# A new order for the 1297 steps of a hand-ordered attention and MLP kernel

## The chip, the cores and the metric

The kernel runs on one core of a Trainium2 chip. Times are device microseconds (us) of one execution. Before the change the median of three runs is 326.21 us (325.22 to 327.37).

## What is computed

Causal attention in a sliding window of 64 positions (8 batches, 8 heads, 576 positions, 64 wide), and behind it an MLP over all 4608 tokens, whose activation is `h - tanh(h)`:

```python
scores = scale * np.matmul(q, k.transpose(0, 1, 3, 2))
rel = pos[:, None] - pos[None, :]
scores = np.where((rel >= 0) & (rel < 64), scores, -1000000000.0)
attn = softmax(scores)
x = (attn @ v).transpose(0, 2, 1, 3).reshape(4608, 512)
h = x @ w_in            # 512 x 2048
out = (h - np.tanh(h)) @ w_out
```

Inputs and output are float32; the kernel multiplies in bfloat16 and adds up in float32.

## The kernel before

The kernel is one string, `PLAN`, of 1297 words. Each word is a step, that is a call of a small function; `play` calls them from left to right, so each engine gets its instructions in the order of the words. A letter behind a step names its engine: `a` ACT (ScalarE), `v` DVE (VectorE), `p` POOL (GpSimd), `s` SP (SyncE, which only issues DMAs). Engines run side by side and wait for each other by semaphores alone; within an engine, and within a queue of DMA issues, a step that waits holds up all behind it.

Heads are worked on in pairs, four to a batch: pair g belongs to batch g // 4. The MLP takes the 4608 tokens in 9 chunks of 512. So attention of later batches lies between the matmuls of the MLP for earlier tokens. The steps:

- Loads. `lk.g`, `lq.g`: K and Q rows of a pair, 144 KB as they arrive (L106); the first two go through SP as float32, the others through GpSimd, which converts on the way. `lv.b.r.h`, `lt.b`: V of one head, 64 KB (L145, L140). `LV.b.i`: V rows of 128 positions, all heads, 128 KB (L158). `LQ.b`: all Q of a batch, 576 KB (L112). `lr.b.i.h`: K rows of 128 positions (L174). `wi.0` to `wi.2`: w_in in parts for the hidden blocks 0 to 3, 4 to 7 and 8 to 15 (512, 512 and 1024 KB, L187). `wo.0` to `wo.3`: w_out, 512 KB each (L195).
- Q and K to channels on partitions. Batches 0 to 2: `ck.g`, `cq.g` reorder or convert the rows, `Fp.g`, `Ep.g` transpose them on PE (six matmuls of 96 columns, L258), `Fc.g` copies K out of PSUM, `Ea.g` and `Eb.g` copy the two heads of Q (L86 on ACT, L88 on DVE). From batch 3 on K is transposed by a DMA that SP issues (`tk.b.i`, L179); from batch 6 on Q too, by way of DRAM: `cz.g` spreads the rows on GpSimd (L126), `bo.g` writes them (L131), `td.g` reads them back transposed (L136). The buffers `qT`, which hold a pair's queries, are two: `td.g` waits for the scores of pair g-2.
- Attention. `Rp.g.n.bank`: three score matmuls of 128 columns into a PSUM bank (L286; the first four pairs add the mask with a product of its own, L275). `Rx`: exp on ACT (L291). `M.g`: the mask by a product on DVE (L295), for later pairs; the mask lies in PSUM bank 6. `za`, `zb`, `Z.b`: copies of V between the halves of the partitions. `P.g`, `D.g`: PV and normalisation of one pair (L307, L347, L349); `PP.g`, `DR`, `DN`: the same for two pairs, in banks 5 to 7 (L320, L328, L340). `Xp`, `Xc`: the result transposed on PE and copied to the chunk (L355), or from batch 3 on by a DMA, `Y.b` (L374).
- MLP. `H`: one hidden block of a chunk, four matmuls (L385), into banks 0 and 1 in turn; `A`: tanh on ACT (L392); `G`: the subtraction on DVE (L398), which frees the bank; `W`: a quarter of a down-projection of 128 tokens, four matmuls (L417); `O`: copy to SBUF and output DMA on SP.
- `U.n`: n matmuls of 512 columns of zeros, which keep PE busy (L222). `i`, `h`, `n`, `N`: identity and masks, on GpSimd first. `u`, `mv`, `mq`, `mt`, `mk`, `z`: cleared buffers.

Of the kernel before, what the change touches and what calls it, by code (L numbers as in the profile page):

```python
# [15 lines left out]
def kernel(  # L16
# [48 lines left out]
    NR, NPT, NROW = 2, 4, 3  # L65
    hidden_by_product = range(4)
# [181 lines left out]
    def tr(g, which, bank):  # L248
        tp = ps[:, bank, :].bitcast(BF16)[:, 0:E * P].rearrange("c (e p) -> c e p", e=E)
        if (g, which) not in rows:  # L250
            src = stage.pop((g, which))
            for h in range(2):
                for e in range(E):
                    nc.tensor.transpose(tp[64 * h:64 * h + 64, e, :], src[:, h, 64 * e:64 * e + 64], ident[:P, :P])
            return
        src = rows.pop((g, which)).rearrange("p e h d -> p e (h d)")
        for e in range(E):
            nc.tensor.transpose(tp[:, e, :], src[:, e, :], ident[:P, :P])  # L258

    def put(g, which, bank, eng):  # L260
        t = ps[:, bank, :].bitcast(BF16)[:, 0:E * P].rearrange("c (e p) -> c p e", e=E)
        if which == "c":
            move(eng, qp[g % NR].rearrange("c (p e) -> c p e", e=E), t)
        elif which == "k":
            move(eng, kT[g % NR][:, 64:].rearrange("c (p e) -> c p e", e=E), t)
        else:
            h = "ab".index(which)
            r = slice(64 * h, 64 * h + 64)
            move(eng, qT[g % NR].rearrange("c h (p e) -> c h p e", e=E)[r, h], t[r])

    def scores(g, grp, bank):
        sp = ps[:, bank, 0:384].rearrange("p (i q) -> p i q", i=3)
        first = g not in hidden_by_product
        if not first:
            nc.tensor.matmul(sp, ident, hide.rearrange("p h t -> p (h t)").unsqueeze(1).to_broadcast([128, 3, 128]),  # L275
                             start=True, stop=False)
        for i in range(3):
            j = 3 * grp + i
            kt = kT[g % NR] if g // NP not in K_BY_DMA else kw[g // NP % 2][:, g % NP]
            if g // NP in BY_HEAD:  # L280
                for h in range(2):
                    r = slice(64 * h, 64 * h + 64)
                    nc.tensor.matmul(sp[:, i, r], kt[r, 64 * j:64 * j + 128], qp[g % NR][r, 64 * j:64 * j + 64],
                                     start=first, stop=first or (i == 2 and h == 1))
                continue
            nc.tensor.matmul(sp[:, i, :], kt[:, 64 * j:64 * j + 128], qT[g % NR][:, :, 64 * j:64 * j + 64],  # L286
                             start=first, stop=first or i == 2)
# [9 lines left out]
    def pv_banks(g):  # L297
        return ps[:, 4:8:3, :] if g < NP and g % 2 else ps[:, 5:7, :]
# [83 lines left out]
    def hp_mm(c, m):  # L382
        hp = ps[:, m % 2 if c > 1 else m % 3, :]
        for ki in range(4):
            nc.tensor.matmul(hp, w_in_tile(ki, m),  # L385
                             chunk_tile(c)[:, :, ki % 2, 64 * (ki // 2):64 * (ki // 2) + 64],
# [53 lines left out]
    def step(what):  # L440
        i = count[what]
        count[what] += 1
        c, m = divmod(i, 4 if what == "O" else M)
        return c, m

    def first_layer():
        c, m = step("H")
        hidden[c, m] = hp_mm(c, m)

    def tanh():  # L450
        k = step("A")
        hidden[k] = squash(hidden[k])

    def subtract():
        c, m = step("G")
        g_sub(c, m, *hidden.pop((c, m)))
# [11 lines left out]
        Fc=lambda g, k, e: put(g, "k", k, e), Ea=lambda g, k, e: put(g, "a", k, e), Ec=lambda g, k, e: put(g, "c", k, e), Eb=lambda g, k, e: put(g, "b", k, e),  # L468
        Rp=scores, Rx=probs, M=masking, za=cross_low, zb=cross_high, Z=cross_rows,
# [3 lines left out]
    def play(script):  # L473
# [5 lines left out]
        lk.0.s lq.0.s i h n u U.6 mq.1 mv.1 mv.0 ck.0.v cq.0.a mq.0 mt.0 Fp.0.2 U.2 Fc.0.2.a Ep.0.3 U.2  # L479
        Eb.0.3.v Ea.0.3.a Rp.0.0.0 lk.2.p lq.2.p lq.1.p lk.3.p cq.2.a Rx.0.0.0 Rp.0.1.1 U.2 Rp.0.2.0  # L480
        lv.0.2.1 lt.0 lv.0.2.0 mt.1 ck.2.v Fp.2.2 Ep.2.3 Fc.2.2.v Eb.2.3.v lk.1.p ck.1.v lk.4.p lv.0.3.0
        lv.0.1.0 lq.3.p lq.5.p lv.0.1.1 lv.0.3.1 lk.5.p Rx.0.2.0 Ea.2.3.a Rx.0.1.1 cq.1.a lv.0.0.1 lv.0.0.0
        lq.4.p lk.6.p wi.0 wi.1 lq.6.p wi.2 lq.7.p lv.1.1.0 lv.1.1.1 lt.1 lv.1.0.0 lv.1.0.1 lk.7.p wo.0 N
        U.5 Rp.2.2.0 Rp.2.1.1 Rx.2.1.1 Rx.2.2.0 Ep.1.3 Eb.1.3.a Fp.1.2 U.1 Rp.2.0.0 U.2 Rx.2.0.0 ck.3.a
        Ea.1.3.v Fc.1.2.v ck.4.v za.0.2.v zb.0.2.v Rp.1.0.1 Rx.1.0.1 Rp.1.1.0 P.2 Rp.1.2.1 cq.3.a Fp.3.2
        Ep.3.3 D.2 Rx.1.2.1 Eb.3.3.a Ea.3.3.a Rx.1.1.0 Fp.4.3 za.0.1.v cq.5.v zb.0.1.v Fc.3.2.v Rp.3.2.1
        Rx.3.2.1 P.1 Rp.3.1.0 ck.5.v zb.0.3.v za.0.3.v zb.0.0.v za.0.0.v Rp.3.0.1 Fc.4.3.a Rx.3.1.0 Rx.3.0.1
        D.1 Ep.5.3 Eb.5.3.a Ea.5.3.a P.0 P.3 D.0 Fp.5.3 Fc.5.3.a Xp.0.0.1.2 Xc.0.0.1.2.a D.3 Xp.0.1.0.3
        Rp.5.2.4 Xp.0.1.1.2 Xc.0.1.0.3.a Rx.5.2.4 Xp.0.0.0.3 Rp.5.1.4 Xc.0.0.0.3.a cq.4.v ck.6.v
        Xc.0.1.1.2.v Ep.4.3 Eb.4.3.a Rx.5.1.4 H H Rp.5.0.4 A Ea.4.3.a Rx.5.0.4 H A G G M.5 Rp.4.0.4 H  # L490
# [89 lines left out]
```

## Time and profile before

| | |
|---|---|
| Median of 3 runs | 326.21 us |
| Profiled execution | 328.84 us |
| its span, first to last instruction | 327.1 us |
| 144 up-projection blocks, L385, PE busy | 142.1 us |
| 35 full down-projections, L417, PE busy | 136.2 us |
| subtraction L398, DVE | 98.4 us in 144 instructions |
| tanh L392, ACT | 85.3 us in 144 |
| exp L291, ACT | 46.1 us in 96 |
| HBM | 36.70 MB read, 11.80 MB written |

"Busy" is the time that at least one instruction of the engine was under way, so a busy PE need not be at its best rate: four matmuls of 512 columns in a row take 0.86 us where nothing holds them up. A DMA's issue takes its queue's engine some time (0.64 to 0.8 us on GpSimd), and it lands later. The chain of waits, the work that ended last, traced back from the end, lies on PE for 71% of the span and on DMA for 14%.

### The profile page before, as it was taken

Reading aid. Unit: us, or ns where it says so; the run is one execution under the profiler, and the core shown is the slowest. Engines: PE = TensorE matmul, PEld = TensorE weight load, DVE = VectorE, ACT = ScalarE, POOL = GpSimd, SP = SyncE. Lnnn points to the kernel's source line nnn. Section 1 sums busy time; section 2 is a strip of 40 time slices with the busy share of each in tenths; the row PEclk is TensorE's granted clock in tenths of the full one; section 3 lists DMA queues with packets and bytes.
Section 4 is the critical chain, followed back from the end, with each engine's and each line's share of the span. In section 5 each row is a group of like instructions: output and inputs, shape, how many; then the busy total and the mean of one; then the engine's idle time right before and its main releaser. Section 6 shows DMA issues by size and latency. Waiting matters only on the chain.

```text
span 327.1 us, 5992 instructions
## 1 busy us (share of the span) xinstructions
PE 307.7 (94%) x2343; PEld 167.8 (51%) x2343; DVE 196.3 (60%) x337; ACT 175.3 (54%) x326; POOL 112.2 (34%) x166
## 2 busy tenths in 40 slices
PE   7858999999899999999999995999999999999995
PEld 2546555556555545555555552555554444444444
DVE  5384895889868886857585561566384445344400
ACT  3677875489866775665564452455433344443300
POOL 8892648577696169490503330000000000000000
PEclk9997999999999999999999998999999999999999
DMA  7999999999999999699994999144004010000121
GB/s 130 147 139 207 170 205 159 169 164 122 144 163 167 127 134 170 81 141 209 144 192 111 148 197 202 36 107 103 34 32 106 32 64 32 35 32 32 34 93 67
DMA packets 113196, 39.09 MB, mean 119 GB/s; under 512 B 96400, under 2 KB 107664, under 8 KB 113168
## 3 DMA queue, kind: packets, MB, share of 16 engines
q0 software_dynamic: 72128, 18.06, 64.6%
q1 hardware_dynamic: 41040, 20.65, 28.9%
q8 instruction: 18, 0.29, 0.4%
q14 instruction: 10, 0.08, 0.1%
HBM read 36.70 MB, written 11.80 MB: 148 GB/s over the span
## 4 chain that ended last, share of the span: by engine, by line
PE 71%; DMA 14%; POOL 5%; DVE 3%; ACT 3%; issue 2%; POOLq 0%; DVEq 0%; ACTq 0%
PE ps L417 32%; PE ps L385 31%; DMA kall<-in_k_dram 6%; DMA vw<-in_v_dram 5%; PE ps L286 3%; DMA xT<-xs 2%; PE ps L320 2%; DMA qt<-qd 1%; POOL qall L106 1%; POOL kall L106 1%; PE ps L411 1%; ACT th L392 1%; PE ps L258 1%; DVE gT L398 1%; DVE pt L295 1%
## 5 line engine op out<-in xcount | busy, mean ns | idle before, releaser
L398 DVE TENSOR_TENSOR gT<-ps,th 128x512 bf16<-128x512 f32 x144 | 98.4, 689 | 83.4 <-ACT th L392 82.2
L385 PE MATMUL ps<-xT,wi 128*128 128x512 bf16 x576 | 142.1, 382 | 2.2 <-DVE gT L398 1.8
L417 PE MATMUL ps<-w_out_sb,gT 128*128 128x512 bf16 x560 | 136.2, 380 | 0.0
L392 ACT ACTIVATE th<-ps 128x512 f32<-128x512 f32 x144 | 85.3, 597 | 76.0 <-PE ps L385 74.9
L385 PEld LDWEIGHTS <-wi 128*128 128x128 bf16 x576 | 62.5, 114 | 52.6 <-issue 3.8
L417 PEld LDWEIGHTS <-gT 128*128 128x128 bf16 x560 | 53.2, 98 | 57.3 <-issue 1.1
L291 ACT ACTIVATE pt<-ps 128x384 bf16<-128x384 f32 x96 | 46.1, 488 | 27.4 <-PE ps L286 27.0
L174 POOL DMA_DIRECT2D kall<-in_k_dram x50 | 37.5, 764 | 9.5 <-DMA qall<-in_q_dram 2.7
L158 POOL DMA_DIRECT2D vw<-in_v_dram x30 | 25.7, 866 | 31.5 <-PE ps L320 22.0
L86 ACT ACTIVATE ysb<-ps 128x512 f32<-128x512 f32 (+1 forms) x19 | 10.9, 574 | 28.1 <-PE ps L417 18.7
L86 ACT ACTIVATE qt<-ps 64x576 bf16<-64x576 bf16 x32 | 20.6, 643 | 9.7 <-PE ps L258 6.3
L88 DVE COPY ysb<-ps 128x512 f32<-128x512 f32 x18 | 12.4, 689 | 21.3 <-PE ps L417 21.1
L286 PE MATMUL ps<-qt,kw 128*128 128x128 bf16 x180 | 19.5, 222 | 4.4 <-DMA qt<-qd 3.4
L286 PEld LDWEIGHTS <-kw 128*128 128x128 bf16 x180 | 14.4, 99 | 15.9 <-issue 5.3
L295 DVE TENSOR_TENSOR pt<-pt,ps 128x1152 bf16<-128x1152 bf16 x28 | 20.6, 745 | 1.4 <-PE ps L320 1.0
L340 DVE TENSOR_TENSOR xs<-ps,rcp 128x384 bf16<-128x384 f32 x28 | 14.9, 551 | 0.3
L286 PE MATMUL ps<-qt,kt 128*128 128x128 bf16 x108 | 12.7, 229 | 2.2 <-DVE kt L88 1.0
L145 POOL DMA_DIRECT2D vw<-in_v_dram x16 | 12.2, 773 | 7.0 <-DMA wi<-in_moe_w_in_dram 4.4
L88 DVE COPY qt<-ps 64x576 bf16<-64x576 bf16 x16 | 12.1, 755 | 4.0 <-PE ps L258 1.9
L126 POOL COPY qz<-qall 96x384 bf16<-96x384 bf16 x16 | 7.6, 510 | 18.8 <-DMA qd<-qz 18.7
L286 PEld LDWEIGHTS <-kt 128*128 128x128 bf16 x108 | 9.1, 104 | 8.7 <-issue 2.7
L258 PE MATMUL ps<-ident,qb 96*128 96x96 bf16 x144 | 10.6, 212 | 1.2 <-DVE qb L88 0.4
(61 smaller groups left out, 175.9 us busy)
## 6 DMA issues: line engine op xcount, KB each, us to landing
out_dram<-ysb SPq DMA_DIRECT2D x35, 256.0 KB, 2.3
vw<-in_v_dram POOLq DMA_DIRECT2D x24, 128.0 KB, 6.0
qall<-in_q_dram POOLq DMA_DIRECT2D x5, 576.0 KB, 9.3
kall<-in_k_dram POOLq DMA_DIRECT2D x40, 64.0 KB, 5.4
qd<-qz SPq DMA_DIRECT2D x8, 288.0 KB, 3.8
w_out_sb<-in_moe_w_out_dram POOLq DMA_DIRECT2D x4, 512.0 KB, 8.2
kall<-in_k_dram POOLq DMA_DIRECT2D x11, 144.0 KB, 5.3
qall<-in_q_dram POOLq DMA_DIRECT2D x11, 144.0 KB, 5.3
```

What stands on the lines that cost most here:

```text
L86: nc.scalar.activation(o, i, ACT.Copy)
L88: eng.tensor_copy(o, i)
L158: nc.gpsimd.dma_start(out=w[:, 2 * i + 1, :, 0:D] if i < NF else w[64:128, 2 * i, :, 0:D], in_=v[b, :, 128 * i:128 * i + n].rearrange("h p ...
L174: nc.gpsimd.dma_start(out=token_rows(b)[0:c, i, :, h, :], in_=k[b, NP * h:NP * h + NP, 128 * i:128 * i + c].rearrange("r p d -> p r d"))
L286: nc.tensor.matmul(sp[:, i, :], kt[:, 64 * j:64 * j + 128], qT[g % NR][:, :, 64 * j:64 * j + 64], start=first, stop=first or i == 2)
L291: nc.scalar.activation(PT[g % NPT][:, 3 * grp:3 * grp + 3, :], sp, ACT.Exp, scale=scale)
L295: nc.vector.tensor_tensor(p, p, mask.unsqueeze(1).to_broadcast([128, 2 * NJ, 64]), ALU.mult)
L340: nc.vector.tensor_tensor(xs[b % 2][:, 0:6, p0 + n // 2, :], ov[:, :, 0:D], sums[g][:, n].to_broadcast([128, 6, D]), ALU.mult)
L385: nc.tensor.matmul(hp, w_in_tile(ki, m), chunk_tile(c)[:, :, ki % 2, 64 * (ki // 2):64 * (ki // 2) + 64], start=(ki == 0), stop=(ki == 3))
L392: nc.scalar.activation(th, hp, ACT.Tanh)
L398: nc.vector.tensor_tensor(gT[c][:, m, :], hp, th, ALU.subtract)
L417: nc.tensor.matmul(yp, gT[c][:, m, s * 128:(s + 1) * 128], w_out_sb[:, m, :], start=(m == 0), stop=(m == M - 1))
```

## The change

Each step's function does what it did, and all 1297 words are still there, but for the letter of their engine at 57 places and the number of zero products (`U`: 6+2+2+2+5+1+2 before, 9+3+5+1+4+7+3 after). Their order is another from the first word to the last. GpSimd, which made identity and masks (`i h n`) ahead of its first load, now starts with `lk.1`, makes `i` and `h` between loads, and `n` after the loads of w_in. SP's two first loads change places. The pairs of batch 0 come in the order 0, 1, 3, 2 rather than 0, 2, 1, 3. Four V copies go from DVE to GpSimd.

New functions for half a batch (`half_*`), for scores by head (`group`), and the split of the first hidden blocks are switched off by `SPLIT = 0` and `BY_HEAD = ()`; no word of the plan calls them. The diff, without them; of the plan the start, the place of `LV.2` and that of `td.28`:

```diff
     NR, NPT, NROW = 2, 4, 3
+    SPLIT = 0
+    NKR = 4 if SPLIT else NR
...
     def warm_up(n, bank=5):
+        w = 3 if bank == 6 else 4
         for i in range(n):
-            nc.tensor.matmul(ps[:, bank, :], warm, warm.unsqueeze(1).to_broadcast([128, 4, 128]), start=True, stop=True)
+            nc.tensor.matmul(ps[:, bank, 0:128 * w], warm, warm.unsqueeze(1).to_broadcast([128, w, 128]), start=True, stop=True)
...
-            for h in range(2):
-                for e in range(E):
+            for e in range(E):
+                for h in range(2):
                     nc.tensor.transpose(tp[64 * h:64 * h + 64, e, :], src[:, h, 64 * e:64 * e + 64], ident[:P, :P])
...
     PLAN = """
-        lk.0.s lq.0.s i h n u U.6 mq.1 mv.1 mv.0 ck.0.v cq.0.a mq.0 mt.0 Fp.0.2 U.2 Fc.0.2.a Ep.0.3 U.2
-        Eb.0.3.v Ea.0.3.a Rp.0.0.0 lk.2.p lq.2.p lq.1.p lk.3.p cq.2.a Rx.0.0.0 Rp.0.1.1 U.2 Rp.0.2.0
-        lv.0.2.1 lt.0 lv.0.2.0 mt.1 ck.2.v Fp.2.2 Ep.2.3 Fc.2.2.v Eb.2.3.v lk.1.p ck.1.v lk.4.p lv.0.3.0
-        lv.0.1.0 lq.3.p lq.5.p lv.0.1.1 lv.0.3.1 lk.5.p Rx.0.2.0 Ea.2.3.a Rx.0.1.1 cq.1.a lv.0.0.1 lv.0.0.0
-        lq.4.p lk.6.p wi.0 wi.1 lq.6.p wi.2 lq.7.p lv.1.1.0 lv.1.1.1 lt.1 lv.1.0.0 lv.1.0.1 lk.7.p wo.0 N
-        U.5 Rp.2.2.0 Rp.2.1.1 Rx.2.1.1 Rx.2.2.0 Ep.1.3 Eb.1.3.a Fp.1.2 U.1 Rp.2.0.0 U.2 Rx.2.0.0 ck.3.a
-        Ea.1.3.v Fc.1.2.v ck.4.v za.0.2.v zb.0.2.v Rp.1.0.1 Rx.1.0.1 Rp.1.1.0 P.2 Rp.1.2.1 cq.3.a Fp.3.2
-        Ep.3.3 D.2 Rx.1.2.1 Eb.3.3.a Ea.3.3.a Rx.1.1.0 Fp.4.3 za.0.1.v cq.5.v zb.0.1.v Fc.3.2.v Rp.3.2.1
-        Rx.3.2.1 P.1 Rp.3.1.0 ck.5.v zb.0.3.v za.0.3.v zb.0.0.v za.0.0.v Rp.3.0.1 Fc.4.3.a Rx.3.1.0 Rx.3.0.1
-        D.1 Ep.5.3 Eb.5.3.a Ea.5.3.a P.0 P.3 D.0 Fp.5.3 Fc.5.3.a Xp.0.0.1.2 Xc.0.0.1.2.a D.3 Xp.0.1.0.3
-        Rp.5.2.4 Xp.0.1.1.2 Xc.0.1.0.3.a Rx.5.2.4 Xp.0.0.0.3 Rp.5.1.4 Xc.0.0.0.3.a cq.4.v ck.6.v
-        Xc.0.1.1.2.v Ep.4.3 Eb.4.3.a Rx.5.1.4 H H Rp.5.0.4 A Ea.4.3.a Rx.5.0.4 H A G G M.5 Rp.4.0.4 H
-        Rx.4.0.4 A G A Fp.6.3 Rp.4.2.4 Rx.4.2.4 H A cq.6.v G G Rp.4.1.4 H H H Fc.6.3.a A A A Rx.4.1.4 wo.1
-        wo.2 wo.3 zb.1.1.p Ep.6.3 G G G H H H A A A M.4 G G H H A A Eb.6.3.a cq.7.v G G G lk.9.p lk.8.p
...
-        lr.3.1.0 lr.3.0.1 lq.9.p LQ.3 LV.2.3 lr.3.4.0 lr.3.2.1 LV.2.1 LV.2.2 lr.3.4.1 lr.3.2.0 LV.2.0 LV.2.4
-        lr.3.1.1 lr.3.0.0 lr.3.3.0 lr.3.3.1 Ea.7.3.v Eb.7.3.v Rx.6.2.4 DR.4 DN.4.2 DN.4.0 DN.4.1 W Rp.6.1.4
-        Rx.6.1.4 ck.9.v W Rp.7.1.4 Rx.7.1.4 W Rp.7.0.4 Xp.1.0.0.3 Xc.1.0.0.3.a W Xp.1.0.1.3 Rx.7.0.4 W
...
-        W W H H lr.7.0.1 LV.7.2 cz.29 td.27 O.v tk.7.3 W Rp.26.1.3 Rp.26.2.4 W A Rx.26.2.4 Rx.26.1.3 A
-        DN.22.2 G M.25 G Y.5 W H A G Rp.27.1.4 Rp.27.2.3 H A W H Rx.27.1.4 O.v bo.29 G A Rx.27.2.3 Rp.26.0.4
-        PP.24 G H A G W H Rp.27.0.3 H Rx.26.0.4 A DR.24 DN.24.0 DN.24.2 W A Rx.27.0.3 cz.28 G G H H W A A G
-        G DN.24.1 bo.28 tk.7.2 tk.7.0 tk.7.1 tk.7.4 td.28 W H LV.7.0 LV.7.1 LV.7.3 cz.31 cz.30 LV.7.4 td.29
-        Rp.28.0.4 Rp.28.1.3 bo.30 bo.31 O.a Rx.28.1.3 Rx.28.0.4 A G H A G W W W H H Rp.29.0.3 A A M.26 M.27
-        G G W O.a H Rp.28.2.4 Rx.28.2.4 W Rp.29.1.4 PP.26 H A A G H W A W Rx.29.1.4 Rx.29.0.3 W Rp.29.2.3
...
+        lq.0.s lk.0.s u U.9 mv.0 mq.0 mv.1 lk.1.p i lq.1.p lk.3.p h lq.3.p lk.2.p ck.0.a cq.0.a ck.1.v
+        cq.1.a mt.0 Fp.0.2 Ep.0.3 Fc.0.2.v mq.1 Ea.0.3.a Eb.0.3.a U.3 Ep.1.3 Rp.0.2.0 Rx.0.2.0 Rp.0.1.1
+        Fp.1.2 mt.1 Fc.1.2.v cq.3.v Rx.0.1.1 lv.0.1.0 lq.2.p cq.2.v lq.4.p lq.5.p lv.0.0.0 lk.5.p lv.0.0.1
+        lt.0 lv.0.3.0 lv.0.1.1 lk.4.p lv.0.3.1 lq.6.p lv.0.2.0 lv.0.2.1 Rp.0.0.0 Ea.1.3.a Eb.1.3.a Rx.0.0.0
+        U.5 Rp.1.2.1 Rx.1.2.1 Rp.1.1.0 Ep.3.3 Rp.1.0.1 ck.2.a U.1 Fp.2.2 Fc.2.2.a Rx.1.0.1 Rx.1.1.0 Ea.3.3.v
+        ck.3.v U.4 Fp.3.2 Eb.3.3.v Ep.2.3 Ea.2.3.v cq.5.a Fc.3.2.a U.7 Rp.3.1.0 Rp.3.0.1 Eb.2.3.a Rx.3.0.1
+        za.0.0.v ck.5.v zb.0.0.v cq.4.v za.0.1.v zb.0.1.v lk.6.p wi.0 zb.0.3.p wi.1 P.0 Fp.5.3 Rp.3.2.1 P.1
+        Rx.3.1.0 Rx.3.2.1 Fc.5.3.a Rp.2.2.0 Rx.2.2.0 Rp.2.1.1 Ep.5.3 D.0 D.1 Rp.2.0.0 Xp.0.0.1.2 Rx.2.1.1
+        Ea.5.3.a ck.4.v za.0.3.v wi.2 zb.0.2.p Eb.5.3.v za.0.2.v n lv.1.1.1 lk.7.p lq.7.p lv.1.0.1 lv.1.0.0
+        lt.1 lq.8.p lv.1.1.0 wo.0 wo.1 P.3 D.3 Rx.2.0.0 U.3.5 P.2 Xp.0.0.0.3 Xc.0.0.1.2.a Xc.0.0.0.3.a D.2
+        Xp.0.1.0.3 Xc.0.1.0.3.v Xp.0.1.1.2 Rp.5.2.4 N Ep.4.3 Xc.0.1.1.2.a H A H A H Ea.4.3.v Rx.5.2.4 A
+        Eb.4.3.v G G G cq.6.v Fp.4.3 Fc.4.3.a H A H Rp.4.2.4 ck.6.a G A Rx.4.2.4 H H A A G G Rp.4.0.4 Fp.6.3
+        Rx.4.0.4 H Rp.4.1.4 Fc.6.3.v H Rx.4.1.4 A A Ep.6.3 Rp.5.0.4 G G G Ea.6.3.a Eb.6.3.v ck.7.v H H H A
+        Rx.5.0.4 A A Rp.5.1.4 Fp.7.3 G cq.7.v G Fc.7.3.v G M.4 H Rx.5.1.4 cq.8.a Rp.6.1.4 Rx.6.1.4 H A A
+        Rp.6.0.4 Ep.7.3 Rx.6.0.4 Ea.7.3.a za.1.0.p lk.8.p zb.1.1.p wo.2 lv.1.3.0 za.1.1.p zb.1.0.p wo.3
...
+        Ea.9.3.a za.1.3.v M.7 za.1.2.v W Rx.8.1.4 PP.6 Rp.8.0.4 ck.9.v lq.10.p lk.11.p lk.10.p LV.2.3 LV.2.2
+        lr.3.2.0 lr.3.3.0 lq.11.p LV.2.4 LQ.3 lr.3.2.1 Eb.9.3.v Fp.9.3 Rx.8.0.4 Fc.9.3.a ck.11.a ck.10.a W W
+        DR.6 DN.6.1 DN.6.0 DN.6.2 Xp.1.1.0.3 Xc.1.1.0.3.v W Rp.9.2.4 cq.10.v M.8 Xp.1.1.1.3 W Rx.9.2.4
+        Xc.1.1.1.3.a LV.2.1 mk LV.2.0 lr.3.3.1 tk.3.2 O.v cq.11.v O.a Rp.9.0.4 Fp.10.3 tk.3.3 lr.3.1.0
...
+        G W W H W td.26 Rx.24.2.4 A A cz.28 LV.7.1 lr.7.3.0 O.a tk.7.3 bo.28 td.27 G G M.25 Y.5 lr.7.1.0 H H
+        W Rp.26.2.4 W A G H A A G G Rx.26.2.4 H W W H cz.29 LV.7.2 LV.7.4 lr.7.0.1 LV.7.0 bo.29 A Z.6 G O.a
+        tk.7.4 tk.7.1 A G Rp.26.0.4 W H Rp.27.0.3 H A A Rx.26.0.4 Rx.27.0.3 W W W Rp.27.1.4 Rp.27.2.3 G G
+        M.24 H O.v H Rx.27.2.3 Rx.27.1.4 A A tk.7.0 cz.30 cz.31 LV.7.3 Rp.26.1.3 PP.24 G H G H A A W G G H H
+        W A A DR.24 DN.24.1 G H W A G H A Rx.26.1.3 G M.27 DN.24.2 DN.24.0 W td.28 bo.30 td.29 bo.31 M.26
+        O.a H Rp.28.1.3 Rp.28.2.4 W W A Rx.28.1.3 Rx.28.2.4 G G PP.26 Rp.29.2.3 H A W Rp.29.1.4 Rx.29.1.4 W
...
```

## The prediction

> **What bounds the kernel now.** I read the page's first two parts, then windows over the stretches with a gap, then the timeline there, then landing times. Columns below: busy and idle tenths, 40 slices.
>
> ```profile
> span 327.1 us, 5992 instructions
> ...
> PE 307.7 (94%) x2343; PEld 167.8 (51%) x2343; DVE 196.3 (60%) x337; ACT 175.3 (54%) x326; POOL 112.2 (34%) x166
> ...
> PE   7858999999899999999999995999999999999995
> ...
> PEclk9997999999999999999999998999999999999999
> DMA  7999999999999999699994999144004010000121
> ```
>
> PE is the bound except in the first four slices (33 us) and in slice 25 (196 to 204 us), where the clock also falls. DMA stands at 9 for nearly 200 us. Busy hides slow matmuls, so I also count: 4 products of the MLP at full rate take 0.863 us, three scores 0.16, six transposes 0.24, PV of two pairs 0.70; every step of the plan together, without warm-up matmuls, makes 288.9 us. The other 38 us of the span are: 20.6 before the first up-projection, 5.1 at 197 to 205, some 8 spread over 32 to 190, 4.5 from the last chunk's end on and rounding. Windows (length; busy time of PE, PEld, DVE, ACT, POOL; clock; DMA):
>
> ```profile
> 10.50:24.00 13.50, 9.53 (x137) 6.51 (x136) 9.44 (x21) 9.88 (x19) 12.24 (x18) 1.00 1.47 142
> 24.00:27.70 3.70, 2.06 (x56) 1.72 (x56) 3.04 (x7) 2.83 (x6) 0.76 (x1) 0.97 1.23 196
> 27.70:31.20 3.50, 3.14 (x26) 2.41 (x24) 0.67 (x3) 2.28 (x5) 1.38 (x2) 0.54 1.14 212
> 196.00:208.00 12.00, 8.55 (x38) 3.94 (x36) 4.16 (x7) 2.98 (x6) 0.00 (x0) 0.86 0.68 142
> ```
>
> In the prologue DVE and ACT are each busy some 70% and PE waits for both; the first up-projection runs at half clock. The timeline there (start, duration, what; in brackets the idle time before and what ended it):
>
> ```profile
> 26.54 0.76 POOL L145 DMA_DIRECT2D vw<-in_v_dram  x1 [2.64 <-DMA wi<-in_moe_w_in_dram]
> ...
> 30.23 2.23 PE L385 MATMUL ps<-xT,wi 128*128 128x512 bf16 x8
> ```
>
> GpSimd's queue is full, so the transfers set its pace. wi.0, issued at 18.08, lands 8.2 us later (26.3), four before PE uses it. SP's queue ahead of the second gap, then PE:
>
> ```profile
> 190.03 7.13 SPq L179 DMA_TRANSPOSE kw<-kall  x4
> 197.27 2.64 SPq L136 DMA_TRANSPOSE qt<-qd  x2
> ```
>
> ```profile
> 201.83 0.80 PE L286 MATMUL ps<-qt,kw 128*128 128x128 bf16 x6 [3.44 <-DMA qt<-qd]
> 202.42 1.92 PE L385 MATMUL ps<-xT,wi 128*128 128x512 bf16 x4
> ```
>
> Pair 28's query transpose (td.28) stands behind four K transposes (tk.7) that took SP 7.13 us.
>
> **The change part by part.** By instruction counts it adds 12 warm-up matmuls (20 to 32), moves four V copies (zb.0.2, zb.0.3, za.1.0, zb.1.0) from DVE to GpSimd and swaps some ten puts and casts between ACT and DVE, whose sums stay within 1 us of what they were. The rest is order. The branches for SPLIT and BY_HEAD are never entered, and every pair is cast first, so the reordered loop in `tr` isn't reached: nothing for these.
>
> *Prologue.* (a) Path of the weights. Before, 20 loads of 2160 KB on GpSimd precede wi.0; the first lands at 6.4 (3.07+3.4), the last, lk.6, at 21.9 (17.27+4.6): 2016 KB in 15.5 us, 130 KB a microsecond. The change puts lq.6 (144 KB, 1.1 us) in front of wi.0 as well, and issues the first load at 0.82 rather than 3.07, since the masks come later. If SP's two loads leave no room early on, nothing of 2.25 us is gained; if all, 2.25. DMA moved 72 GB/s at 4 to 5 us against some 140 later, so part was free: I take 1.4. wi.0 lands at 26.3+1.1-1.4 = 26.0 (25.2 to 27.4). (b) Path of the attention. Pairs now come as 0, 1, 3, 2, and q and k of all four stand in the first 928 KB (before 1328): that takes waits for lk.1 and lq.3 away from the front. Last are pair 2's V halves, after 2160 KB: 21.9-1.4 = 20.5. Then a GpSimd copy 0.61 (row of zb.1.1), PV 0.51, reciprocal and norm 1.05, transposes 0.49, two copies on one engine 1.4, handovers 0.5: 25.1. ACT's own list from the first Rx (9.6 by the rows of pair 0, one cast later than before) to the last score before it is 12 Rx of 0.49, ten puts and casts of 0.65 to 0.83, together 12.8: 22.4, so it fits; DVE's list of 12.8 from 7.6 does too. First up-projection at about 26.2 instead of 30.23: 4.0. One six-transpose group and one score group are put off (0.4): **3.6 saved**, 2.3 to 4.7 by the landing alone. The warm-ups (12 x 0.216, or 0.427 cold) lie in PE's waits; uncovered they would cost 2.6. GpSimd's copies cost nothing, as its queue waits for room behind them (2.64 above); without that cover, 0.61 each.
>
> The clock's rows: at 56% PE busy (24.0 to 27.7) it fell to half for 3.4 us, at 61% just before (2.46 of 4.0) it did not. The Trainium skill ("TensorE: Matmul & The Clock Gate", "What's actually happening") has it fall after an idle window; by that rule a stretch half busy stays fast and the new order would be worth up to 1.7 more. The row decides: I assume one such stretch in either order and gain nothing.
>
> *Pair 28.* I give each step a position: PE work of the steps before it (whole plan 293.2 before, 295.8 after with warm-ups). Before, td.28 stands at 171.8 and its scores at 173.5: 1.7 us for a transfer whose eight rows took 3.0 to 8.0 (median 3.7). After, the qT buffer comes free with Rp.26.1.3 at 168.3, SP has only tk.7.0 (1.25) ahead of it, and the scores stand at 178.7: 10.4 against at most 9.3. The 3.44 go, and 3.4 us at half clock after them (1.7): **5.1 saved**. Late next is td.25: freed at 137.2, used at 143.4, 6.2 us: covered by the median, not by the slowest (1.8 short, 3.5 with the clock); I charge 0.7.
>
> *The body.* PE idle from 44 to 124 is 3.9 us by windows, mostly products waiting for DVE to free a bank. DVE's own steps exceed PE's where positions are 80 to 96 (19.6 us of work in 16); after, 56 to 72 (18.7) and 80 to 96 hold 16.4. From -3.9 (all waits go) to +4 (the same again); nearest is the pair of overloads, 3.6 against 3.1: **0.5 saved**.
>
> Sum: 3.6+5.1-0.7+0.5 = 8.5. The profiled execution (328.84, 1.7 of it outside its span) would be 320.3; it stands 2.63 above the median, so 326.2-8.5 = **317.7**.
>
> **Rivals.** *The loads keep the pace* (0.2). By byte counts lk.7, wi.2, wo.3, lk.10 and lq.11 land 0.3 to 1.6 us before they are needed, so whatever the queue lacks comes straight off PE's lead: the prologue is worth only the 1.4 of the earlier start, 6.3 in all, 319.9. Pair 0 may also be later, as lk.1 now shares the engines with SP's two loads: two loads' service of 2.2 us puts ACT's list at 24.6 and the first product near 27.5. The Trainium skill ("DMA: Bandwidth & Descriptors", "Queues, rings and completion order") says that an engine serves its queues in turn; by that rule it would be so. Against: SP's first load landed 3.3 us after issue and GpSimd's first 3.4, with SP's second still in flight.
>
> *The stall moves to another td* (0.15): td.27 stands behind an output, tk.7.3 and bo.28. Its scores are 9.7 us after that output, of which SP takes 2.1 and the transfer up to 8.0; late by 1 to 2 and with the half clock 1.7 it costs 3.5: 321.2.
>
> *Batch 2's V late: slower* (0.1). LV.2.1 and LV.2.0 now stand behind LQ.3 (576 KB) on GpSimd. Z.2, the copy that needs them, is on DVE, in order, and all subtractions that free PE's banks queue behind it. By bytes LV.2.0 lands where it did (9824 KB, 69.5) or 1.4 earlier; Z.2 comes at 62.2+10 = 72. Every microsecond past that is one of the span; from 12 late (84) the kernel is slower by more than 1%. GpSimd does wait for PE so long: L158's loads stood 22 us behind L320 twice, at worst 17.4. With that wait on LV.2.0: 317.7+17.4-4 = 331. Against: its buffer is free since batch 0.
>
> *Given back* (0.1): DVE's overload at 56 to 72 costs all 2.7 plus 4 of waits: 324.4, no change.
>
> **How the numbers follow.** Forecast 0.45. One percent (3.3 us) is about what a measurement tells from no change. Faster: forecast, loads, and 0.09 of the moved stall, 0.74; same: 0.06 of it and 0.07 of the giving back, 0.13; slower 0.13. Range: low end with all upper values, 4.7+5.1+3.9 = 13.7, 312.5; high end 327, past giving back, leaving the slower case and little else out.
>
> **What would show it.** First L385 product near 26 with wi.0 just landed; L286 after qt<-qd without a gap near 190 to 200; a clock row without the dip there; td.25 and td.27 rows with small waits. Wrong, if the first product is past 28.5, a new PE gap above 3 us stands anywhere past 40, or Z.2 waits for a V load.

## The result and the profile after

The changed kernel takes 336.42 us (median of 4 runs, 333.24 to 338.43), the kernel before 325.94 in the same runs: a ratio of 1.028 (95% interval 1.020 to 1.037), slower. The prediction was 317.7. The profiled execution took 338.43 us, 2 above its median; that of before 328.84, 2.9 above. Medians, here and below, are over all executions, while ratios and intervals leave out slow ones, to which the profiled execution of the changed kernel, the slowest of its four, belongs.

The page of the changed kernel: span, PE, and the 40 slices of 8.4 us.

```profile
span 336.7 us, 6031 instructions
...
PE 314.7 (93%) x2355; PEld 170.0 (50%) x2355; DVE 194.9 (58%) x333; ACT 173.7 (52%) x326; POOL 114.3 (34%) x170
...
PE   6987999999997599999958999999999999999995
...
PEclk9696999999999599999997999999999999999999
DMA  8999999999969999919995999335005000110022
```

The hole at 200 us is gone, as predicted. Two others stand there: slices 13 and 14 (101 to 118 us) and 21 and 22 (168 to 185), each with a fall of the clock behind it. PE's waits of the changed kernel (who waited for what: us in total, times, longest) name them:

```profile
PE ps L300 <- DMA kw<-kall: 5.3, 2, 3.3
PE ps L300 <- DMA qt<-qd: 4.9, 1, 4.9
PE ps L225 <- DVE xs L447: 1.8, 1, 1.8
```

Both large waits are scores (L300) that wait for a DMA transpose from SP: one for batch 4's K (tk.4), one for pair 25's Q (td.25). The third is in the prologue. (After the change H is L489, W L522, scores L300, warm-ups L225, PV of one pair L405, its normalization L447, the transposes of x L453, tk L181, td L138.)

Waits alone don't show slow matmuls, so I take elapsed time less the work of PE at full rate (288.8 us in all, by the durations that the prediction uses): "lost" us by stretch. The traces of the experiments lack some 30 matmul records of the down-projections, spread evenly; these are filled in.

| lost us in | 0-40 | 40-104 | 104-128 | 128-160 | 160-192 | 192-216 | 216-264 |
|---|---|---|---|---|---|---|---|
| before | 20.9 | 4.4 | 2.7 | 0.4 | 0.7 | 5.3 | 0.2 |
| after | 24.4 | 3.7 | 7.9 | 0.6 | 7.0 | 0.2 | 0.5 |
| e1_before_prologue | 21.8 | 4.1 | 6.2 | 0.7 | 7.6 | 0.4 | 0.3 |
| m1_lq5_later | 23.0 | 4.0 | 1.5 | 0.5 | 8.0 | 0.4 | 0.2 |
| m2_tk4_first | 22.7 | 4.2 | 0.7 | 0.5 | 6.8 | 0.4 | 0.4 |
| s1_lq7_later | 23.1 | 4.3 | 5.8 | 0.4 | 4.5 | 0.1 | 0.5 |
| m12s1_all_three | 24.6 | 4.1 | 0.6 | 0.4 | 4.2 | 0.5 | 0.3 |
| n1_batch7_loads_later | 22.1 | 3.9 | 0.5 | 0.4 | 2.8 | 0.1 | 0.3 |
| n3_before_tk7_spread | 20.9 | 4.2 | 2.7 | 0.4 | 0.9 | 0.2 | 0.3 |
| n5_p2_ahead | 20.6 | 3.9 | 0.7 | 0.3 | 1.5 | 0.2 | 0.2 |

The first two rows are the answer in outline: +3.5 in the prologue, -0.7 in the body, +5.2 at tk.4, +6.3 at td.25, -5.1 at td.28, +0.5 elsewhere: 9.7, and the spans differ by 9.6. The two new stalls don't belong to this one execution alone: in the traces of e1, e3, e4 and n6 below, which keep the changed order past the prologue, the scores wait 3.9 to 5.1 us for tk.4 and 4.1 to 5.3 for td.25.

**The stall at 107 us.** SP's timeline of the changed kernel (start, duration, what):

```profile
95.31 0.33 SPq L538 DMA_DIRECT2D out_dram<-ysb  x1
95.75 8.63 SPq L181 DMA_TRANSPOSE kw<-kall  x5
```

and its DMA issues from 95.5 to 104 us (KB of each; median us from issue to landing):

```profile
qall<-in_q_dram POOLq DMA_DIRECT2D x1, 576.0 KB, 10.0
...
kall<-in_k_dram POOLq DMA_DIRECT2D x3, 64.0 KB, 14.3
kw<-kall SPq DMA_TRANSPOSE x5, 10.3
```

The same view of before, 87 to 99 us:

```profile
kall<-in_k_dram POOLq DMA_DIRECT2D x8, 64.0 KB, 5.3
...
kw<-kall SPq DMA_TRANSPOSE x5, 5.5
```

Before, SP issued the five from 88.2 to 98.7 and they landed by 103.7. After, they stand behind an output that comes at 95.3, although their data had landed by 92.9, and on the way they share the DMA engines with LQ.5 (576 KB, issued at 95.1) and the loads behind it: 10.3 us (median) for 5.5, landing at 105.1 to 113.2. The scores ask from 107.6 on.

**The stall at 173 us.** SP's timeline of the changed kernel again:

```profile
155.18 6.24 SPq L472 DMA_TRANSPOSE xT<-xs  x2
161.52 1.20 SPq L181 DMA_TRANSPOSE kw<-kall  x1
162.81 0.56 SPq L538 DMA_DIRECT2D out_dram<-ysb  x1
163.54 2.82 SPq L181 DMA_TRANSPOSE kw<-kall  x2
166.49 4.38 SPq L138 DMA_TRANSPOSE qt<-qd  x1
170.99 1.20 SPq L181 DMA_TRANSPOSE kw<-kall  x1
172.72 2.40 SPq L138 DMA_TRANSPOSE qt<-qd  x1
```

The last line is td.25. Its buffer came free at 167.2, with pair 23's last scores; it was issued 5.6 us later and landed at 178.0, while PE waited from 173.2. In front of it SP lost 6.2 us on Y.4, 4.4 on td.24, and K transposes whose loads stood on GpSimd behind LQ.7, which had itself waited 12.4 us for its buffer (until 151.6).

### The profile page after: what moved, and what is told of

Same layout as the page of the kernel before. It is cut to its first block, busy times and chain, and to the rows that moved or that the text cites. A ratio compares the mean times of both kernels' runs of the same rounds, so it can differ in the third digit from the quotient of the medians.

```text
span 336.7 us, 6031 instructions
## 1 busy us (share of the span) xinstructions
PE 314.7 (93%) x2355; PEld 170.0 (50%) x2355; DVE 194.9 (58%) x333; ACT 173.7 (52%) x326; POOL 114.3 (34%) x170
## 4 chain that ended last, share of the span: by engine, by line
PE 72%; DMA 10%; POOL 4%; DVE 4%; ACT 4%; SPq 2%; issue 2%; POOLq 0%; ACTq 0%; DVEq 0%
PE ps L489 32%; PE ps L522 32%; PE ps L300 3%; DMA kw<-kall 3%; DMA vw<-in_v_dram 3%; SPq L181 2%; PE ps L418 2%; DMA out_dram<-ysb 2%; DMA qt<-qd 2%; POOL vw L147 1%; PE ps L261 1%; DMA qall<-in_q_dram 1%; ACT th L497 1%; PE ps L516 1%; PE ps L453 1%
## 5 line engine op out<-in xcount | busy, mean ns | idle before, releaser
L489 PE MATMUL ps<-xT,wi 128*128 128x512 bf16 x576 | 144.1, 387 | 0.4 <-DVE gT L503 0.2
L522 PE MATMUL ps<-w_out_sb,gT 128*128 128x512 bf16 x560 | 135.8, 381 | 0.0
L489 PEld LDWEIGHTS <-wi 128*128 128x128 bf16 x576 | 63.4, 115 | 54.2 <-issue 5.2
L522 PEld LDWEIGHTS <-gT 128*128 128x128 bf16 x560 | 53.2, 98 | 56.6 <-issue 1.8
L176 POOL DMA_DIRECT2D kall<-in_k_dram x50 | 36.7, 743 | 22.3 <-DMA vw<-in_v_dram 10.1
L300 PE MATMUL ps<-qt,kw 128*128 128x128 bf16 x180 | 19.8, 221 | 10.3 <-DMA kw<-kall 5.3
L90 DVE COPY ysb<-ps 128x512 f32<-128x512 f32 (+1 forms) x16 | 10.8, 674 | 30.6 <-PE ps L522 29.6
L88 ACT ACTIVATE ysb<-ps 128x512 f32<-128x512 f32 (+1 forms) x21 | 12.4, 588 | 25.5 <-PE ps L516 13.3
L300 PEld LDWEIGHTS <-kw 128*128 128x128 bf16 x180 | 14.1, 98 | 22.2 <-issue 6.4
L88 ACT ACTIVATE qt<-ps 64x576 bf16<-64x576 bf16 x30 | 19.2, 641 | 4.3 <-PE ps L261 3.3
L393 DVE TENSOR_TENSOR pt<-pt,ps 128x1152 bf16<-128x1152 bf16 x28 | 20.6, 740 | 0.6 <-ACT pt L305 0.5
L90 DVE COPY qt<-ps 64x576 bf16<-64x576 bf16 x18 | 13.6, 757 | 8.2 <-ACT pt L305 2.9
L128 POOL COPY qz<-qall 96x384 bf16<-96x384 bf16 x16 | 7.8, 524 | 25.7 <-DMA qd<-qz 24.4
L147 POOL DMA_DIRECT2D vw<-in_v_dram x16 | 12.4, 775 | 4.4 <-DMA wi<-in_moe_w_in_dram 4.4
L225 PE MATMUL ps<-warm 128*128 128x512 bf16 x32 | 10.9, 481 | 2.9 <-DVE xs L447 1.8
L300 PE MATMUL ps<-qt,kt 128*128 128x128 bf16 x108 | 12.9, 232 | 0.0
```

The lines of the kernel that those rows point to most:

```text
L88: nc.scalar.activation(o, i, ACT.Copy)
L90: eng.tensor_copy(o, i)
L147: eng.dma_start(out=vw[b % 2][:, 1::2, h, 0:D], in_=v[b, h, 0:128 * NF].rearrange("(i p) d -> p i d", p=128))
L176: nc.gpsimd.dma_start(out=token_rows(b)[0:c, i, :, h, :], in_=k[b, NP * h:NP * h + NP, 128 * i:128 * i + c].rearrange("r p d -> p r d"))
L300: nc.tensor.matmul(sp[:, i], kt[:, 64 * j:64 * j + 128], qT[g % NR][:, :, 64 * j:64 * j + 64], start=first, stop=first or i == n - 1)
L393: nc.vector.tensor_tensor(p, p, mask.unsqueeze(1).to_broadcast([128, 2 * NJ, 64]), ALU.mult)
```

## The experiments

Where a label has no diff of its own, words of `PLAN` are moved as the text says. Ratios are to the kernel before, run beside it.

**e1_before_prologue, e2_after_prologue**: the words that a kernel has ahead of its first `H`, put into the order, on the engines and with the warm-ups of the other kernel, both ways.

```diff
-        lq.0.s lk.0.s u U.9 mv.0 mq.0 mv.1 lk.1.p i lq.1.p lk.3.p h lq.3.p lk.2.p ck.0.a cq.0.a ck.1.v
+        lk.0.s lq.0.s i h n u U.6 mq.1 mv.1 mv.0 ck.0.v cq.0.a mq.0 mt.0 Fp.0.2 U.2 Fc.0.2.a Ep.0.3 U.2
...
```

Expected of e1:

> The changed kernel, but everything that its plan puts ahead of the first up-projection stands in the order, on the engines and with the warm-up matmuls of before; the rest as changed. Theory A (the new prologue itself is slow, 3.5 us of lost PE time more than before by 40 us; two other losses stand on their own at 107-117 and 173-182): about 3 us faster than the changed kernel, 330 to 334, first L489 product near 30.2. Theory B (only one cause: the later transfers are late because the plan asks for them late, and PE waits there for whatever it gained before): within 1 us of the changed kernel, 335 to 337, and the gap at 107 grows by what the start gains.

Expected of e2:

> The kernel before, with the changed kernel's prologue alone (all that stands ahead of the first up-projection). Theory A: about 3 us slower than before, 328 to 331, first L385 product near 32. Theory B: as before, 325 to 327, since the rest has slack of its own.

Measured: e1 335.84 (1.029, 1.026 to 1.031), no different from the changed kernel, and e2 334.81 (1.020, 1.002 to 1.038). So the prologue is not where the 10 us are. Two readings were left: three separate losses, or a fixed amount of late transfers that PE meets later if not sooner. The second run is spoiled as evidence by a stall of 5.1 us of its own (the last section).

**e3_v_copies_on_dve** (`zb.0.3.p` and `zb.0.2.p` to `.v`), **e4_no_warm_up_5** (without `U.3.5`):

Expected of e3:

> The changed kernel with the V copies zb.0.2 and zb.0.3 back on DVE, in the places where they stand. In the changed trace a DVE cast of 0.35 us took 1.13 while GpSimd copied V (20.6 to 21.7). If the two engines get in each other's way there: casts at 0.35 again, two more copies of 0.35 on DVE, the first product about 0.5 us earlier, 335.5 to 336.5. If GpSimd's copies cost nothing, as the prediction had it: DVE has 0.7 more to do and the start is that much later, 336.5 to 337.5. In both cases under 1 us.

Expected of e4:

> The changed kernel without the three warm-up matmuls in PSUM bank 5 (U.3.5), which in the changed trace wait 1.84 us for the normalisation of pair 3 and hold back PV of pair 2. If these are what delays the start: PV of pair 2 at about 26.4 instead of 28.15, first product near 30.5 instead of 32.1, 334 to 335.5; the clock may fall all the same. If PV of pair 2 waits for the same normalisation by itself (it writes banks 5 and 6): PV at 27.4, first product near 31.4, 335.5 to 336.5.

Measured: e3 337.17 (1.032, 1.024 to 1.040) and e4 336.44 (1.030, 1.019 to 1.040): neither the copies on GpSimd nor the warm-up costs anything that shows in the time, which could hide 1 us. In e4's trace pair 2's PV still waits 1.9 us for pair 3's normalization, but the first product comes at 31.0 and not 32.1: the three warm-up matmuls stand behind that wait, not in it.

**m1_lq5_later**: one load of GpSimd, 14 words later. **m2_tk4_first**: the five transposes ahead of the output (and two loads that they read, further up).

```diff
-        lr.4.1.1 LQ.5 tk.4.1
+        lr.4.1.1 tk.4.1
...
-        lr.5.4.1 lr.5.1.1
+        lr.5.4.1 lr.5.1.1 LQ.5
```

```diff
-        Rp.12.2.4 O.a Rx.12.2.4
+        Rp.12.2.4 tk.4.2 tk.4.3 tk.4.0 tk.4.4 tk.4.1 O.a Rx.12.2.4
...
-        tk.4.2 tk.4.3 lr.4.0.1 tk.4.0 tk.4.4 lr.5.1.0 lr.4.1.1 LQ.5 tk.4.1
+        lr.5.1.0 LQ.5
```

Expected of m1:

> The changed kernel with one of GpSimd's loads moved: LQ.5 (the 576 KB of batch 5's Q) is issued behind that round's K and V loads instead of ahead of them. Theory crowding: batch 4's K transposes land late (105.1 to 113.2 us) because bulk loads share the DMA engines with them; with LQ.5 later each lands some 1 to 3 us earlier, PE's stall of 3.3 + 2.0 us near 107 to 111 us shrinks by that, the K loads behind LQ.5 no longer wait its 4.4 us, and the time is 333 to 335 us. Theory order: the transposes are late because SP issues them behind an output, 8 us later than before; moving one load changes nothing at 107 us and the time stays 336 to 337 us.

Expected of m2:

> The changed kernel with batch 4's five K transposes ahead of the second output on SP's queue (and the two loads that they read moved up on GpSimd's). Theory order: they are issued before 95 us, when their data have landed (92.9 us at the latest), and land by 104 us; the two scores waits at 107 to 111 us and the half clock behind them go, 5 us less lost there, and the time is 331 to 332 us, unless PE then meets the same loss at a later landing (fixed budget: 335 to 337 us). Theory crowding: issued earlier they still take 8 to 9 us to land, the stall is only partly gone, 334 us.

Measured: m1 331.46 (1.015, 1.006 to 1.024) and m2 329.97 (1.012, 1.005 to 1.020). These intervals overlap or touch the changed kernel's (1.020 to 1.037); the traces are clearer. Either edit is enough: 7.9 lost us at 104 to 128 become 1.5 and 0.7. The DMA issues of m1_lq5_later, 94.5 to 101.5 us, and of m2_tk4_first, 86 to 94 us:

```profile
kw<-kall SPq DMA_TRANSPOSE x5, 8.2
```

```profile
kw<-kall SPq DMA_TRANSPOSE x5, 4.1
```

In m1 they are issued nearly as late as in the changed kernel (from 94.6 on, for 95.7) and are still slow, but the last lands at 107.3 and not 113.2, and the scores wait 0.7 us. In m2, issued from 86.4 on, they land by 94.9. So the stall had two causes that were both needed: issued late, and slowed by bulk loads. The waits did not come back later, against the fixed amount: td.25 lost 8.0 and 6.8 for 7.0.

**s1_lq7_later**: LQ.7 behind the K and V loads that it held up.

```diff
-        LQ.7 lr.6.1.1 tk.6.1
+        lr.6.1.1 tk.6.1
...
-        lr.7.2.0 td.25
+        lr.7.2.0 LQ.7 td.25
```

> The changed kernel with LQ.7 (Q of batch 7, whose buffer comes free only after GpSimd has waited 12.4 us) issued behind the K and V loads that now stand behind it. Theory queue: these loads go 10 us earlier, SP's tk.6.1 and tk.6.0 no longer come late, td.24 and td.25 are issued near 160 and not 166 to 175 us, and the 5.1 us wait of the scores at 172.8 and the half clock behind it (6.9 us lost in all) go: 329 to 331 us. Theory fixed budget: PE waits elsewhere for what it gains here, 335 to 337 us. If SP's own issue times (4.5 us for Y.4, 4.4 for td.24) are what makes td.25 late and not the loads, the wait shrinks by less than 2 us: 334 to 336 us.

Measured: 332.66 (1.022, 1.011 to 1.034). The wait at td.25 falls from 4.9 to 2.3 us, not to nothing: td.24 and td.25 go at 160.8 and 169.2 instead of 166.5 and 172.7, and td.24 still holds SP for 5.0 us. That is about half of the expected gain, and the interval overlaps the changed kernel's; a part of the cause lay on SP's own queue.

**m12s1_all_three**: m1, m2 and s1 in one.

> All three moves together. If the losses at 107 and at 173 us are separate and each falls to its move: 12 us lost at those two places in the changed kernel, so 324 to 327 us, with the 3.5 us of the prologue still lost against the kernel before. If a fixed budget of late transfers decides: 333 us or more.

Measured: 325.64 (0.995, 0.990 to 1.000), 10.8 below the changed kernel and level with the kernel before. With most of the two stalls gone the whole net loss is gone; what its trace still loses at 160 to 192 (4.2 for 0.7) and up to 40 (24.6 for 20.9), pair 28 makes up for.

**n1_batch7_loads_later**: on top of it batch 7's loads behind batch 6's V, and td.25 ahead of tk.6.0. **n2_before_prologue_too**: that with the prologue of before. **n3_before_tk7_spread**: the kernel before, with only this:

```diff
-        cz.27 lr.7.1.0 lr.7.3.0 Rx.23.2.4
+        cz.27 lr.7.1.0 lr.7.3.0 lr.7.0.1 Rx.23.2.4
...
-        bo.26 A
+        bo.26 tk.7.2 tk.7.1 A
...
-        td.26 O.a
+        td.26 O.a tk.7.0
...
-        O.v tk.7.3
+        O.v tk.7.4 tk.7.3
...
-        bo.28 tk.7.2 tk.7.0 tk.7.1 tk.7.4 td.28
+        bo.28 td.28
```

**n4_v_copies_on_dve**: n1 with the two V copies on VectorE.

Expected of n1:

> The kernel with all three moves (325.6 us), in which the scores still wait 2.4 us for td.25 at 166 us, with 1.7 us of half clock behind it. Here batch 7's loads (seven of 0.4 to 0.6 MB) go behind batch 6's V and two SP steps, and td.25 goes ahead of tk.6.0. Theory crowding and queue: tk.6.1, tk.6.2 and td.24 land within 3 to 5 us and not 9, td.25 lands before 166 us, the wait and its half clock go: 321 to 323 us. Theory fixed budget: the loads then come late for pair 28 (tk.7.x behind lr.7.x) and PE waits near 195 to 205 us for what it gained: 325 to 327 us.

Expected of n2:

> The same with the prologue (all that stands ahead of the first up-projection, order and engines) of the kernel before. Theory three losses: once no later transfer eats it, the prologue of before is worth what the traces put between the two (first product 1 to 2 us earlier, one window of half clock, 1.7 us, less): 2 to 3.5 us below the run without it, so 318.5 to 321 us. Theory fixed budget: no difference, as between the changed kernel and the run of it with the prologue of before (336.4 and 335.8).

Expected of n3:

> The kernel before, with batch 7's K transposes spread over SP's idle time (two behind bo.26, one behind the thirteenth output, one ahead of tk.7.3) so that td.28 stands behind none of them; lr.7.0.1 moves up for it. That is pair 28's stall removed by itself, without the rest of the change. Theory: td.28 is issued near 190 us, as pair 26's last scores (188.6) allow, and lands by 194; the wait of 3.6 us at 198 and the half clock behind it, 1.7, go: 320 to 322 us. If transposes issued earlier crowd td.26 or td.27 instead: 325 us.

Expected of n4:

> The kernel of the first of these four runs, with the two V copies that the change gave to GpSimd back on VectorE. Theory port (VectorE's casts beside GpSimd's copies took 1.13 us for 0.35): VectorE's chain to the last normalization gets 1 to 2 us shorter though it has two copies more, the first product comes as much earlier, and the time is 1 to 2 us lower, half or more of what the whole prologue of before brings. If the two extra copies cost what they gain: the same within 0.5 us.

Measured: n1 324.63 (0.995, 0.992 to 0.998), n2 324.78 (0.995, 0.992 to 0.999), n3 323.77 (0.990, 0.986 to 0.993), n4 325.89 (0.999, 0.996 to 1.001). n1 gains less than expected, since a wait of 1.7 us at td.25 stays (GpSimd, no longer blocked, issued the moved loads at the same time as ever). n2 missed: even without later stalls the old prologue is worth nothing. n4 missed too: it is no faster than n1, so nothing here shows that VectorE and GpSimd hold each other up in the prologue. n3 shows pair 28's stall alone, worth some 3 us of the 5 expected; SP's timeline there has td.28 and td.29 free of transposes in front of them:

```profile
189.44 0.89 SPq L131 DMA_DIRECT2D qd<-qz  x2
193.65 2.59 SPq L136 DMA_TRANSPOSE qt<-qd  x2
```

and PE's timeline has the scores of pair 28 at 198.38 without a wait in front:

```profile
198.38 0.50 PE L286 MATMUL ps<-qt,kw 128*128 128x128 bf16 x6
```

By then the cause of the prologue's late first product was still open. The traces had PE waiting for pair 3's normalization `D.3` ahead of pair 2's PV, though the two use different PSUM banks (4 and 7; 5 and 6). Why the program makes it wait stays open. **n5_p2_ahead** (on n1) and **n6_after_p2_ahead** (on the changed kernel) put `P.2` ahead of it:

```diff
-        P.3 D.3 Rx.2.0.0 U.3.5 P.2 Xp.0.0.0.3
+        P.3 Rx.2.0.0 U.3.5 P.2 D.3 Xp.0.0.0.3
```

**n7_batch7_k_behind_wait**: on n5, six K loads of batch 7 behind `cz.28`, which waits for bo.26, and tk.7.2 beside tk.7.3.

Expected of n5:

> The kernel n1_batch7_loads_later (324.6 us) with pair 2's warm-up and PV put ahead of pair 3's normalization in the order, as the kernel before has it for its last two pairs. Theory order of PV and normalization: PE no longer waits 1.8 us for pair 3's normalization at 23 to 25 us; the two normalizations follow each other on VectorE, the last one ends near 26.5 and not 28.1, and the first product comes 1.5 to 2 us earlier, at 28 to 28.7 us: 322.5 to 323.5 us. Theory loads or clock: PE waits as long for something else (pair 2's V copy, half clock) and the first product stays at 30 us: 324.6 us.

Expected of n6:

> The changed kernel itself (336.4 us) with the same edit. If the order of PV and normalization is the cause of the late first product: first product 1.5 to 2 us earlier than the 29.7 to 32.2 us of its prologue so far. In time, theory fixed budget: batch 4's K transposes land when they land, so the scores at 107 us wait that much longer and the time stays 335.5 to 337 us, as with the whole prologue of before; theory separate losses: 334.5 to 335 us.

Expected of n7:

> As n5_p2_ahead, and the six K loads of batch 7 that GpSimd issues at 146 to 151 us stand behind its wait for bo.26 (near 165 us), with tk.7.2 moved beside tk.7.3. Theory crowding: tk.6.1, tk.6.2 and td.24 land in 3 to 5 us and not 4 to 9, td.25 lands before the scores ask for it (163 us) and their last wait of 1.9 us goes: 1.5 to 2 us below n5_p2_ahead, 320.5 to 322 us. Theory that V loads and Q suffice to crowd: no change at td.25. If the K loads now come late for tk.7: a new wait of pair 28's scores near 197 us, 324 us or more.

Measured: n5 323.29 (0.987, 0.982 to 0.993), n6 335.00 (1.026, 1.022 to 1.030), n7 323.07 (0.989, 0.984 to 0.993). VectorE's timeline of the changed kernel has pair 2's other V copy and, behind it, pair 3's normalization (L447):

```profile
25.90 0.35 DVE L90 COPY vw<-vw 64x520 bf16<-64x520 bf16 x1
...
26.54 0.82 DVE L447 TENSOR_TENSOR xs<-ps,rc 128x640 bf16<-128x640 f32 x1
```

PE's timeline of the changed kernel, from pair 3's PV to the first product:

```profile
24.91 0.67 PE L405 MATMUL ps<-vw,pt 128*64 128x65 bf16 x20
27.42 0.81 PE L225 MATMUL ps<-warm 128*128 128x512 bf16 x3 [1.84 <-DVE xs L447]
28.15 0.74 PE L405 MATMUL ps<-vw,pt 128*64 128x65 bf16 x20
...
32.12 0.63 PE L489 MATMUL ps<-xT,wi 128*128 128x512 bf16 x1
```

and of n5_p2_ahead:

```profile
24.73 0.82 PE L225 MATMUL ps<-warm 128*128 128x512 bf16 x3
25.48 0.51 PE L405 MATMUL ps<-vw,pt 128*64 128x65 bf16 x20
...
28.15 0.68 PE L453 MATMUL ps<-ident,xs 128*128 128x128 bf16 x9 [1.84 <-DVE xs L447]
...
29.39 0.81 PE L489 MATMUL ps<-xT,wi 128*128 128x512 bf16 x3
```

From the start of P.0 (20.6 and 20.2) to the first product it is 11.5 us in the changed kernel, 11.4 to 12.6 in six more runs of its order, and 9.2, 9.3 and 8.9 in n5, n6 and n7. So this order costs 2 to 3 us of the prologue. It is not all: at 29.4, 28.7 and 27.8 us the first product is still later than the 26.2 of the forecast. Against n1 the two intervals just overlap; n6's time can't be told from the changed kernel's, but its scores wait 5.1 us for tk.4 and 4.1 for td.25, no longer than there (5.3 and 4.9): the gain of the prologue isn't met again as a wait, against the fixed amount.

n7 agrees with crowding: with the six loads out of the way td.24 and td.25 land 5.0 and 3.4 us after their issue, for 7.4 and 4.0 in n5, and td.25's wait is gone. Instead td.26, issued at 165.8 just behind the moved loads (from 163.7 on), takes 8.0 us for 7.0, and td.27 is issued only at 177.7, behind two K transposes. PE's timeline has two new small waits, one for each:

```profile
173.82 0.33 PE L300 MATMUL ps<-qt,kw 128*128 128x128 bf16 x3 [0.98 <-DMA qt<-qd]
...
182.43 0.33 PE L300 MATMUL ps<-qt,kw 128*128 128x128 bf16 x3 [1.20 <-DMA qt<-qd]
```

n3, n5 and n7 are some 1% below the kernel before, clear of the noise but small; which of the three is best can't be told.

## Why the prediction was wrong, step by step

- *Path of the weights: right.* wi.0 was to land at 26.0; it landed at 25.0 (24.0 to 26.4 over all runs of the new order).
- *Path of the attention: wrong.* Its two ends hold. Pair 2's V copy was put at 21.1 and ended at 21.5; from pair 2's PV to the first product 3.95 us were summed up, and it took 3.97 (28.15 to 32.12). That this comes out so exactly is luck: nearly all of it ran at half clock, which the sum left out (PV took 0.74 for 0.51). Between the two ends the prediction put nothing: "Last are pair 2's V halves". In the trace 6.6 us lie there. VectorE came to pair 2's other V copy only at 25.9, behind two normalizations (which P.0 and P.1, from 20.6 on, let start) and three copies; "DVE's list of 12.8 from 7.6 does too" counted the work, not this wait. And in the order pair 2's PV stands behind pair 3's normalization, which ended at 27.4. n5, n6 and n7 take that last part away, and 2 to 3 us with it.
- *The prologue's price.* Predicted 3.6 saved. By traces 23.3 us are lost up to 40 (mean of seven runs of the order, 22.1 to 24.6) against 21.6 (four, 20.9 to 22.9); by medians nothing either way (n1 and n2; the changed kernel and e1).
- *GpSimd's copies cost nothing: right* as far as the times can tell (e3, n4). *The warm-ups lie in PE's waits: wrong for the three of `U.3.5`.* They took 0.73 us between the end of the wait and pair 2's PV (27.42 to 28.15); without them (e4) it is 10.2 us from P.0 to the first product and not 11.5. In the time of the whole kernel this did not show.
- *One stretch of half clock in the prologue in either order: right within its scatter*, 6.8 us after, 3.4 to 10.2 in four runs of the old prologue. Past the prologue each new stall brought its own as well: 6.8 us behind tk.4's and 3.4 behind td.25's, half of which is lost.
- *Pair 28, 5.1 saved: right.* Lost at 192 to 216: 5.3, then 0.2. n3, which does this alone, has the same 5.1 in the traces and 1.0% (0.7 to 1.4) in the times, some 3 us.
- *td.25, 0.7 charged: wrong, 6.3.* The step weighed the 6.2 us between buffer and use against the transfer alone ("covered by the median"). The transfer took 5.2, as it might; but SP issued it 5.6 us after the buffer was free. For td.28 the prediction had counted SP's queue; here it did not look at what stood in front, nor that LQ.7's wait on GpSimd held the loads behind it.
- *tk.4: no term at all, 5.2.* The steps moved across SP's queue were priced for `td` only. The list of landings against uses ended at the prologue's loads, `LV.2` and the `td`s; batch 4's K transposes, issued by SP 7.5 us later than before (95.7 for 88.2), were on no list. The prediction's own positions would have shown them: they stand 13 us of PE work ahead of pair 16's first scores in the plan before, and 2 us after (73.4 and 86.3; 84.4 and 86.3).
- *The body, 0.5 saved: right in size* (4.4 to 3.7 at 40 to 104), but no more than the scatter there: 3.7 to 4.3 in the table's traces of the new order.
- *Rivals.* Batch 2's V caused no wait. "The loads keep the pace" did not happen; the Trainium skill's rule named there ("DMA: Bandwidth & Descriptors", "Queues, rings and completion order", an engine serves its queues in turn) would fit what happened elsewhere: tk.4's five transposes took 10.3 us beside GpSimd's loads, 8.2 with LQ.5 behind them and 4.1 with few. These show that bulk loads slow small transfers; no run here shows that it is by turns. "The stall moves to another td" was the right kind of story with the wrong td and about half the price. Two signs set for "wrong", a first product past 28.5 and a new gap above 3 us past 40, both came.

Put together: the forecast had 8.5 us saved, the traces have 9.6 lost. Of the 18.1 between them the prologue is 7.1 (3.6 saved, 3.5 lost), td.25 5.6 and tk.4 5.2. The range ended at 327 because the only slower rival was left out of it, and none had K transposes that come later than before.

## What to carry to other kernels

Where an order is changed as a whole, list for every DMA that feeds the bounding engine its issue, landing and use, in both orders, and count what stands ahead of it on its queue, the waits of those steps included. Bulk loads that nothing needs soon belong behind the small transfers that somebody waits for: here one load moved by 14 words was worth 4 to 5 us. A chain is not priced by its last link's data; ask which step of another chain stands in front of it in program order.

## What the runs showed of the hardware

- The clock goes by how busy PE was in a stretch of 3.41 us, not by the size of one stall. In all 17 traces every stretch of half or full clock between two changes is a multiple of 3.41 us long, so each trace can be cut into windows of that length. Of the windows at full clock, all 33 in which PE was busy for 44% or less were followed by half clock, none of the 1455 with 59% or more was, and 12 of the 19 between. So a stall of 1.8 us among other waits (n1, 23.2 to 25.0) cost 6.8 us of half clock, one of 1.7 alone (n1, 163.6) none, 2.2 (m12s1) 3.4 us, and those of 4.1 to 5.3 at td.25 3.4 or 6.8, by how the windows cut them. In the changed kernel the half clock of 110.13 came after a window in which PE was still busy for 0.84 us. The Trainium skill ("TensorE: Matmul & The Clock Gate", "What's actually happening") tells of idle windows of about 3.4 us; the length agrees, but the window need not be empty.
- One order of the prologue is not always equally quick. Where the half clock of the first 15 us lasted to 14.1 us or later, P.0 began at 20.2 to 20.8 (five traces); where it ended by 12.8, at 18.3 to 19.5 (eight). So single profiles whose prologues differ by less than some 2 us can't be told apart.
- e2_after_prologue met a stall of 5.1 us at 124 us that no other kernel has. VectorE's copies of V there, and GpSimd beside them:

```profile
122.00 5.78 DVE L166 COPY vw<-vw 64x2080 bf16<-64x2080 bf16 x1
127.79 0.97 DVE L167 COPY vw<-vw 64x2080 bf16<-64x2080 bf16 x1
```

```profile
119.92 4.59 POOL L176 DMA_DIRECT2D kall<-in_k_dram  x6
124.48 2.74 POOL L235 MEMSET qz<- 96x1536 bf16 x2
```

  The first copy takes 5.78 us, the second, just as large, 0.97; the first ends 0.6 us after GpSimd's memsets do. The Trainium skill ("SBUF — State Buffer", "SBUF: two separate sides") says that a port pair which VectorE and GpSimd share is locked for a whole instruction. This one trace agrees in part: the copy was held up over several GpSimd instructions, not one. No run here tries it by itself.
- What holds SP at a query transpose for up to 5.6 us (4.4 at td.24, though its buffer had been free since 160.8) stays open; it was 2.8 in n7, where fewer loads were under way.
